# Loads in the order of need, weights behind block 2, eight blocks of lookahead, mask building interleaved: sliding-window attention with a highway layer

## The chip, the cores and the metric

The kernel runs on one core of one Trainium2 chip. The metric is the device time of one execution in microseconds (us). A run also has a span, the time from its first to its last instruction in the trace; here it is about 1.7 us shorter than the device time. Every execution is labelled fast or slow; on one core, slow means over 1.5% above the fastest execution of the same kernel. Medians are over all executions, which takes in three slow ones: one of e5 and two of the kernel before beside e9 to e12.

Engines: PE does matmuls (PEld is its weight load), DVE is the vector engine, ACT the scalar engine, POOL (Pool in the text) the engine that here issues all loads but the small bias row, SP the one that issues the stores. A load is issued by an instruction and lands later, when the trace shows its data complete. PE is called cold where four transposes take 0.61 to 0.63 us in these traces, and warm where they take 0.39 to 0.40 us.

## The reference, cut to what matters

```python
# q, k, v: [4, 8, 768, 64] float32; n_sink = 4, window = 128
scores = q @ k^T / 8
keep   = (key < 4) | (0 <= query - key < 128)       # four sink keys and a window of 128
a      = softmax(where(keep, scores, -1e9))
x      = (a @ v) as [3072, 512]                      # tokens x (8 heads x 64)
H      = relu(x @ w_h)                               # w_h, w_t: [512, 512]
T      = sigmoid(x @ w_t + b_t)
out    = T * H + (1 - T) * x                         # float32
```

## The kernel before

The 3072 tokens are 24 blocks of 128. A load moves 128 tokens of all heads of q, k or v from float32 in memory to float16 on the chip (128 KB written); each weight is 512 KB. In the main loop PE, DVE and ACT follow the program's order (`manual_schedule`); Pool's queue, and everything in front of the loop, is ordered by the scheduler of the framework.

```python
sd_pool = ctx.enter_context(tc.tile_pool(name="p_sd", bufs=6))      # q and k as loaded
NV = 6
v_ring = [const.tile([P, VW], FP16, tag=f"v{i}") for i in range(NV)]  # VW = 8*65 + 64 = 584

load(0)                                   # q and k of block 0
make_identity(nc, ident)                  # on Pool
for vt in v_ring:
    nc.vector.memset(vt, 2.0)             # DVE; column 64 of each head stays 2.0 (row sums)
load_v(0); load(1)
nc.gpsimd.memset(mask, 1.0)               # then two affine_select on Pool, copies on DVE
...
load_v(1)
nc.gpsimd.dma_start(out=wt_sb, in_=moe_w_t...)    # both weights
nc.gpsimd.dma_start(out=wh_sb, in_=moe_w_h...)
... # bias row, sink helpers: small DVE and Pool work

with tc.manual_schedule(engines={ENG.PE, ENG.DVE, ENG.Activation}):
    for i in range(-2, NB + 1):
        if 2 <= i + 4 < NB:
            load(i + 4); load_v(i + 4)
        s = i + 1
        ... stage_sink(i)       # sink scores, for even i
        ... stage_S(s)          # scores of block s: PE, exponential on ACT
        ... stage_A(i)          # probabilities x v of block i
        ... stage_T(i + 2)      # PE transposes q and k, ACT copies qT, DVE copies kT
        ... stage_mask(s)       # DVE
        ... stage_Mt(i - 1)     # x @ w_t, tanh
        ... stage_X(i)          # transposes x
        ... stage_sink_setup
        ... stage_Mh(i - 1)     # x @ w_h, the rest of the highway layer, store
```

T(n), S(n), A(n), Mt(n) and Mh(n) below are these stages for block n; q2 is the q load of block 2, and so on. In PE's order, block 2 is transposed right after A(0), block 3 after A(1), and Mt(0) and Mh(0), the first users of the weights, follow T(3).

The softmax here doesn't subtract the row's maximum and nothing guards it: scores larger than these inputs give would overflow.

Of the kernel before, what the change touches and what calls it, by code (L numbers as in the profile page):

```python
# [9 lines left out]
FP16 = mybir.dt.float16  # L10
FP32 = mybir.dt.float32
AF = mybir.ActivationFunctionType
ALU = mybir.AluOpType
ENG = mybir.EngineType
# [7 lines left out]
def kernel(  # L22
# [18 lines left out]
    nc = tc.nc  # L41
    P = 128

    B, H, S, D = q.shape
    NSINK = int(n_sink)
# [4 lines left out]
    NT, DM = out.shape  # L50
# [4 lines left out]
    NB = NT // P  # L55
    NHP = H // 2
    NOC = DM // P
    SCALE = 1.0 / math.sqrt(D)
    VW = H * 65 + 64

    const = ctx.enter_context(tc.tile_pool(name="const", bufs=1))
    sd_pool = ctx.enter_context(tc.tile_pool(name="p_sd", bufs=6))
    qkT_pool = ctx.enter_context(tc.tile_pool(name="p_qkT", bufs=5))
    e_pool = ctx.enter_context(tc.tile_pool(name="p_e", bufs=5))
    es_pool = ctx.enter_context(tc.tile_pool(name="p_es", bufs=2))
# [5 lines left out]
    av_ps = ctx.enter_context(tc.tile_pool(name="ps_av", bufs=1, space=bass.MemoryType.PSUM))  # L71
    m_ps = ctx.enter_context(tc.tile_pool(name="ps_m", bufs=2, space=bass.MemoryType.PSUM))

    NV = 6
    v_ring = [const.tile([P, VW], FP16, tag=f"v{i}", name=f"v{i}") for i in range(NV)]
    qk_sd = {}

    def load(n):
        b, c = divmod(n, NSC)
        rows = slice(c * P, (c + 1) * P)  # L80
        qsd = sd_pool.tile([P, H, D], FP16, tag="qsd", name="qsd")
        ksd = sd_pool.tile([P, H, D], FP16, tag="ksd", name="ksd")
        nc.gpsimd.dma_start(out=qsd, in_=q[b, :, rows, :].transpose([1, 0, 2]))  # L83
        nc.gpsimd.dma_start(out=ksd, in_=k[b, :, rows, :].transpose([1, 0, 2]))  # L84
        qk_sd[n] = (qsd, ksd)

    def load_v(n):
        b, c = divmod(n, NSC)
        rows = slice(c * P, (c + 1) * P)
        vt = v_ring[n % NV][:, 0:H * 65].rearrange("p (h e) -> p h e", e=65)  # L90
        nc.gpsimd.dma_start(out=vt[:, :, 0:D], in_=v[b, :, rows, :].transpose([1, 0, 2]))
# [1 line left out]

    ebias = const.tile([P, 1], FP32, tag="ebias")
    nc.vector.memset(ebias, _EXP_BIAS)
    load(0)
    ident = const.tile([P, P], FP16, tag="ident")
    make_identity(nc, ident)
    for vt in v_ring:
        nc.vector.memset(vt, 2.0)  # L100
    load_v(0)
    load(1)


    mask = const.tile([P, 2, P], FP16, tag="mask", name="mask")
    nc.gpsimd.memset(mask, 1.0)
    nc.gpsimd.affine_select(
        out=mask[:, 1, :], in_=mask[:, 1, :], compare_op=ALU.is_ge, fill=0.0,
        base=0, pattern=[[1, P]], channel_multiplier=-1)
    nc.gpsimd.affine_select(  # L110
        out=mask[:, 0, :], in_=mask[:, 0, :], compare_op=ALU.is_ge, fill=0.0,
        base=-1, pattern=[[-1, P]], channel_multiplier=1)

    mask1 = const.tile([P, 2, P], FP16, tag="mask1", name="mask1")
    nc.vector.tensor_copy(out=mask1, in_=mask)
    nc.vector.memset(mask1[0:NSINK, 0, :], 1.0)
    mask0 = const.tile([P, P], FP16, tag="mask0", name="mask0")
    nc.vector.tensor_copy(out=mask0, in_=mask[:, 1, :])
    nc.vector.memset(mask0[0:NSINK, :], 1.0)

    load_v(1)
    wh_sb = const.tile([P, NOC, DM], FP16, tag="wh")
    wt_sb = const.tile([P, NOC, DM], FP16, tag="wt")
    nc.gpsimd.dma_start(out=wt_sb, in_=moe_w_t.rearrange("(kc p) of -> p kc of", p=P))
    nc.gpsimd.dma_start(out=wh_sb, in_=moe_w_h.rearrange("(kc p) of -> p kc of", p=P))


    bt32 = const.tile([1, DM], FP32, tag="bt32")
# [11 lines left out]
    for hh in range(2):  # L140
        nc.vector.tensor_copy(
            out=sel[:, :, 4 * hh:4 * hh + NSINK],
            in_=ident[:, 0:NSINK].unsqueeze(1).to_broadcast([P, NHP, NSINK]))
    bdm = const.tile([P, H], FP32, tag="bdm")
    nc.gpsimd.memset(bdm, 1.0)
    bdm3 = bdm.rearrange("p (a b) -> p a b", b=2)
    nc.gpsimd.affine_select(
        out=bdm3, in_=bdm3, compare_op=ALU.is_ge, fill=0.0,
        base=0, pattern=[[-32, NHP], [-4, 2]], channel_multiplier=1)
    nc.gpsimd.affine_select(  # L150
        out=bdm3, in_=bdm3, compare_op=ALU.is_ge, fill=0.0,
        base=NSINK - 1, pattern=[[32, NHP], [4, 2]], channel_multiplier=-1)
    ks_bd = []
    for i in range(2):
        t = const.tile([P, NHP * 160], FP16, tag=f"ks{i}", name=f"ks{i}")
# [11 lines left out]
    def stage_T(n):  # L167
        qsd, ksd = qk_sd.pop(n)
        tp = m_ps.tile([P, 2 * NHP, P], FP16, tag="m", name="tp")
        for j in range(NHP):  # L170
            nc.tensor.transpose(tp[:, j, :], qsd[:, 2 * j:2 * j + 2, :], ident)  # L171
        for j in range(NHP):
            nc.tensor.transpose(tp[:, NHP + j, :], ksd[:, 2 * j:2 * j + 2, :], ident)  # L173
        qT = qkT_pool.tile([P, NHP, P], FP16, tag="qT", name="qT")
        kT = qkT_pool.tile([P, NHP, P], FP16, tag="kT", name="kT")
        nc.scalar.copy(out=qT, in_=tp[:, 0:NHP, :])  # L176
        nc.vector.tensor_copy(out=kT, in_=tp[:, NHP:2 * NHP, :])  # L177
        qkT[n] = (qT, kT)

    def stage_sink_setup(b):  # L180
# [8 lines left out]
        vps = av_ps.tile([P, 2, 512], FP32, tag="av", name="vps")  # L189
        vt = v_ring[(b * NSC) % NV]  # L190
        for g in range(2):
# [11 lines left out]
    def stage_sink(n):  # L203

        b = n // NSC
        ks = ks_bd[b % 2]
        sk = m_ps.tile([P, 2, P], FP32, tag="m", name="sk")
        for t in range(2):
            qT, _ = qkT[n + t]
            for hp in range(NHP):  # L210
                nc.tensor.matmul(sk[:, t, :], lhsT=ks[:, hp * P:(hp + 1) * P],  # L211
                                 rhs=qT[:, hp, :], start=(hp == 0), stop=(hp == NHP - 1))
        es = es_pool.tile([P, 2, P], FP16, tag="es", name="es")
        nc.scalar.activation(out=es, in_=sk, func=AF.Exp, bias=ebias, scale=SCALE)  # L214
        es_of[n] = es_of[n + 1] = es

    def stage_S(n):
        c = n % NSC
        qT, kT = qkT[n]
        srcs = ([] if c == 0 else [qkT[n - 1][1]]) + [kT]  # L220
        np_ = len(srcs)
        es = []
        for g in range(2):
            sps = s_ps.tile([P, 2, 512], FP32, tag="s", name="sps")
            for hl in range(2):
                hp = 2 * g + hl
                for pc, kk in enumerate(srcs):
                    for hh in range(2):
                        rows = slice(64 * hh, 64 * hh + 64)
                        o = (hl * np_ + pc) * P  # L230
                        nc.tensor.matmul(sps[:, hh, o:o + P], lhsT=kk[rows, hp, :],  # L231
                                         rhs=qT[rows, hp, :], start=True, stop=True)
            e = e_pool.tile([P, 2, 2, np_, P], FP16, tag="e", name="e")
            nc.scalar.activation(out=e.rearrange("p a b c d -> p a (b c d)"),  # L234
                                 in_=sps[:, :, 0:2 * np_ * P], func=AF.Exp,
                                 bias=ebias, scale=SCALE)
            es.append(e)
        e_of[n] = (es, np_)

    def stage_mask(n):  # L240
        c = n % NSC
        es, np_ = e_of[n]
        m = {0: mask0, 1: mask1.rearrange("p a b -> p (a b)")}.get(
            c, mask.rearrange("p a b -> p (a b)"))
        for e in es:
            ev = e.rearrange("p a b c d -> p (a b) (c d)")
            nc.vector.tensor_tensor(  # L247
                out=ev, in0=ev, in1=m.unsqueeze(1).to_broadcast([P, 4, np_ * P]),
                op=ALU.mult)

    def stage_A(n):
        b, c = divmod(n, NSC)
        es, np_ = e_of.pop(n)
        vts = ([] if c == 0 else [v_ring[(n - 1) % NV]]) + [v_ring[n % NV]]
        av = av_ps.tile([P, 2, 4, P], FP32, tag="av", name="av")
# [66 lines left out]

    with tc.manual_schedule(engines={ENG.PE, ENG.DVE, ENG.Activation}):
        for i in range(-2, NB + 1):
            if 2 <= i + 4 < NB:
                load(i + 4)
                load_v(i + 4)
            s = i + 1
            if 0 <= i < NB and i % NSC >= 2 and i % 2 == 0:
                stage_sink(i)  # L330
            if 0 <= s < NB:
                stage_S(s)
            if 0 <= i < NB:
                stage_A(i)
            if i + 2 < NB:
                stage_T(i + 2)
            if 0 <= s < NB:
                stage_mask(s)
            if 0 <= i - 1 < NB:
                stage_Mt(i - 1)  # L340
            if 0 <= i < NB:
                stage_X(i)
            if 0 <= i < NB and i % NSC == 0:
                stage_sink_setup(i // NSC)
            if 0 <= i - 1 < NB:
                stage_Mh(i - 1)
# [35 lines left out]
```

## Time and profile before

| | before |
|---|---|
| time, median of 3 runs | 144.44 us (144.27 to 144.75) |
| span of the profiled run | 143.0 us |
| PE / DVE / ACT / Pool busy | 80 / 80 / 63 / 47% of the span |
| a block in the steady part | 4.85 us (29.1 us per six blocks) |

First the page of the kernel before: the span in 40 slices of 3.6 us, each digit the busy share in tenths.

```profile
PE   0345046999999969999999699999997999999730
DVE  6825007588989899989898999899889998999690
DMA  1999999999999998999999999999869021011111
```

PE and DVE stand mostly at 8 or 9 from slice 9 on: from there the blocks follow each other at the pace of the engines. Counted from 1, the hole is in slice 5 for PE and in slices 5 and 6 for DVE: PE stands from 13.4 to 19.1 us, DVE from 14.3 to 21.2 us. The DMA row stands at 9 for most of the span, which looks like a kernel bound by its loads, but that row says only that the DMA engines had work, and the waits have to say whether anybody stood still for it.

The second view is PE's timeline of the kernel before: start, duration, engine, line, instruction, out<-in, number merged; in brackets the idle time before it and what ended it.

```profile
4.87 0.61 PE L171 MATMUL tp<-ident,qsd 128*128 128x128 f16 x4 [4.87 <-DMA qsd<-in_q_dram]
8.86 0.61 PE L231 MATMUL sps<-qT,kT 64*128 64x128 f16 x8 [1.93 <-DVE kT L177]
12.43 0.93 PE L262 MATMUL av<-v_91,e 128*128 128x112 f16 x8
19.10 0.61 PE L171 MATMUL tp<-ident,qsd 128*128 128x128 f16 x4 [5.74 <-DMA qsd<-in_q_dram]
...
26.99 1.44 PE L298 MATMUL tps<-wt_sb,xT 128*128 128x512 f16 x4
28.49 1.03 PE L310 MATMUL hps<-wh_sb,xT 128*128 128x512 f16 x4
```

After A(0) (the `av` line) PE waits 5.74 us for q2. Why q2 is late is in Pool's timeline of the kernel before, which shows when each load is issued:

```profile
6.53 0.91 POOL L91 DMA_DIRECT2D v_92<-in_v_dram  x1
...
7.91 0.79 POOL L124 DMA_DIRECT2D wt_sb<-in_moe_w_t_dram  x1
8.68 0.77 POOL L125 DMA_DIRECT2D wh_sb<-in_moe_w_h_dram  x1
...
9.45 0.92 POOL L83 DMA_DIRECT2D qsd<-in_q_dram  x1
...
10.50 0.94 POOL L84 DMA_DIRECT2D ksd<-in_k_dram  x1
```

Both weights are issued in front of q2. The trace has w_t landing 7.4 us and w_h 9.5 us after issue, so q2 follows at 19.1 us. The last view is DVE's timeline of the kernel before:

```profile
1.03 0.55 DVE L100 MEMSET v_91<- 128x584 f16 x1
...
4.11 0.55 DVE L100 MEMSET v_96<- 128x584 f16 x1
...
7.78 0.27 DVE L118 COPY mask_126<-mask 128x128 f16<-128x128 f16 x1 [1.12 <-POOL mask L107]
...
8.45 0.35 DVE L177 COPY kT<-tp 128x512 f16<-128x512 f16 x1
```

Six memsets of v buffers, 0.615 us from start to start, and other constants stand in front of the first copy of kT, which releases the first scores at 8.86 us.

The chain of waits of the kernel before, followed back from its end, has the columns start, duration, and what the time went to. Three of its lines:

```profile
10.50 9.38 DMA ksd<-in_k_dram
...
60.51 1.11 ACT e L234
...
89.61 1.11 ACT e L234
```

The first is the one long stretch of DMA in it, the wait behind the weights. The other two are the same ACT exponential, six blocks apart, 29.1 us, with no load in the chain between them: in the steady part nobody waits for loads.

### The profile page before, as it was taken

What the parts mean: (1) busy time and instruction counts of PE and PEld (TensorE: products, weight loads), DVE (VectorE), ACT (ScalarE), POOL (GpSimd) and SP (SyncE); (2) the same over time, 40 slices, a digit from 0 to 9 for tenths busy, and PEclk for the clock granted to TensorE, in tenths of its full rate; (3) what the DMA queues carried; (4) which work ended last, traced back from release to release, by engine and by line L of the source; (5) the groups of instructions that cost most, each with busy time, mean ns of one, the idle gap of its engine ahead of it and who ended that gap; (6) DMA issues with size and microseconds to landing.
All of it is one profiled execution on the core that took longest, in us unless ns stands there. A gap on an engine that the chain in (4) does not pass through costs nothing.

```text
span 143.0 us, 3308 instructions
## 1 busy us (share of the span) xinstructions
PE 114.4 (80%) x1312; PEld 73.8 (52%) x1312; DVE 114.1 (80%) x228; ACT 90.3 (63%) x129; POOL 66.8 (47%) x86
## 2 busy tenths in 40 slices
PE   0345046999999969999999699999997999999730
PEld 0134034775676525756765366567644656675310
DVE  6825007588989899989898999899889998999690
ACT  3056026187787677779766867887759579774310
POOL 6999569719975744376349424753040000000000
PEclk9999999999999999999999999999999999999996
DMA  1999999999999998999999999999869021011111
GB/s 10 112 126 156 161 155 155 155 112 142 150 179 201 163 181 64 155 153 137 131 153 125 160 100 135 146 138 134 113 101 124 0 78 73 14 64 73 73 73 73
DMA packets 79408, 16.98 MB, mean 119 GB/s; under 512 B 75297, under 2 KB 76321, under 8 KB 79394
## 3 DMA queue, kind: packets, MB, share of 16 engines
q0 software_dynamic: 75936, 10.49, 109.1%
q1 hardware_dynamic: 3458, 6.30, 12.7%
q8 instruction: 10, 0.16, 0.4%
q14 instruction: 4, 0.03, 0.1%
HBM read 20.97 MB, written 6.29 MB: 191 GB/s over the span
## 4 chain that ended last, share of the span: by engine, by line
DVE 36%; PE 32%; ACT 10%; DMA 7%; issue 7%; POOL 6%; DVEq 0%; POOLq 0%
PE hps L310 12%; DMA ksd<-in_k_dram 7%; DVE ee L316 6%; DVE otok L319 6%; DVE e L247 6%; DVE dd L313 5%; ACT e L234 5%; DVE xh L277 5%; PE av L262 4%; PE tps L298 4%; PE xtp L286 3%; DVE kT L177 3%; PE sk L211 3%; ACT qT L176 2%; DVE vs L196 2%
## 5 line engine op out<-in xcount | busy, mean ns | idle before, releaser
L234 ACT ACTIVATE e<-sps,ebias 128x1024 f16<-128x1024 f32 (+1 forms) x48 | 47.4, 1039 | 15.7 <-PE sps L231 11.4
L298 PE MATMUL tps<-wt_sb,xT 128*128 128x512 f16 x96 | 25.1, 384 | 0.0
L310 PE MATMUL hps<-wh_sb,xT 128*128 128x512 f16 x96 | 24.6, 378 | 0.6
L83 POOL DMA_DIRECT2D qsd<-in_q_dram x24 | 21.9, 914 | 2.7 <-PE tp L173 1.7
L176 ACT COPY qT<-tp 128x512 f16<-128x512 f16 x24 | 14.0, 585 | 14.1 <-PE tp L173 14.1
L84 POOL DMA_DIRECT2D ksd<-in_k_dram x24 | 22.0, 916 | 2.0 <-DMA wh_sb<-in_moe_w_h_dram 2.0
L262 PEld LDWEIGHTS <-e 128*128 128x128 f16 x352 | 20.4, 100 | 4.2 <-DVE vs L196 1.2
L247 DVE TENSOR_TENSOR e<-e,mask 128x1024 f16<-128x1024 f16 x32 | 20.5, 682 | 0.0
L301 ACT ACTIVATE u<-tps 128x512 f16<-128x512 f32 x24 | 14.4, 600 | 9.0 <-PE tps L298 9.0
L177 DVE COPY kT<-tp 128x512 f16<-128x512 f16 x24 | 10.0, 418 | 12.0 <-ACT qT L176 12.0
L313 DVE SCALAR_TENSOR_TENSOR dd<-hps,xh 128x512 f16<-128x512 f32 x24 | 16.5, 687 | 3.4 <-PE hps L310 3.4
L316 DVE SCALAR_TENSOR_TENSOR ee<-u,dd 128x512 f16<-128x512 f16 x24 | 16.6, 692 | 2.9 <-ACT es L214 0.5
L171 PE MATMUL tp<-ident,qsd 128*128 128x128 f16 x96 | 10.2, 234 | 10.6 <-DMA qsd<-in_q_dram 10.6
L231 PE MATMUL sps<-qT,kT 64*128 64x128 f16 x352 | 15.2, 228 | 2.8 <-DVE kT L177 2.1
L319 DVE SCALAR_TENSOR_TENSOR otok<-xh,ee 128x512 f32<-128x512 f16 x24 | 16.6, 692 | 0.8
L277 DVE TENSOR_TENSOR xh<-av,rec 128x512 f16<-128x512 f32 x24 | 16.6, 691 | 0.8
L231 PEld LDWEIGHTS <-kT 64*128 64x128 f16 x352 | 10.7, 99 | 10.1 <-issue 6.8
L288 ACT COPY xT<-xtp 128x512 f16<-128x512 f16 x24 | 14.0, 583 | 1.2 <-PE xtp L286 0.7
L298 PEld LDWEIGHTS <-xT 128*128 128x128 f16 x96 | 9.6, 100 | 9.1 <-issue 0.8
L310 PEld LDWEIGHTS <-xT 128*128 128x128 f16 x96 | 9.2, 97 | 8.1 <-issue 1.3
L171 PEld LDWEIGHTS <-qsd 128*128 128x128 f16 x96 | 7.4, 104 | 11.2 <-DMA qsd<-in_q_dram 10.8
L286 PEld LDWEIGHTS <-xh 128*128 128x128 f16 x96 | 6.2, 100 | 13.1 <-DVE xh L277 11.5
(66 smaller groups left out, 161.8 us busy)
## 6 DMA issues: line engine op xcount, KB each, us to landing
out_dram<-otok SPq DMA_DIRECT2D x24, 256.0 KB, 2.6
qsd<-in_q_dram POOLq DMA_DIRECT2D x24, 128.0 KB, 4.9
ksd<-in_k_dram POOLq DMA_DIRECT2D x24, 128.0 KB, 5.3
v_91<-in_v_dram POOLq DMA_DIRECT2D x4, 128.0 KB, 4.2
v_92<-in_v_dram POOLq DMA_DIRECT2D x4, 128.0 KB, 3.9
wt_sb<-in_moe_w_t_dram POOLq DMA_DIRECT2D x1, 512.0 KB, 7.4
wh_sb<-in_moe_w_h_dram POOLq DMA_DIRECT2D x1, 512.0 KB, 9.5
v_93<-in_v_dram POOLq DMA_DIRECT2D x4, 128.0 KB, 5.3
```

Source lines behind the costliest of these rows:

```text
L83: nc.gpsimd.dma_start(out=qsd, in_=q[b, :, rows, :].transpose([1, 0, 2]))
L84: nc.gpsimd.dma_start(out=ksd, in_=k[b, :, rows, :].transpose([1, 0, 2]))
L231: nc.tensor.matmul(sps[:, hh, o:o + P], lhsT=kk[rows, hp, :], rhs=qT[rows, hp, :], start=True, stop=True)
L234: nc.scalar.activation(out=e.rearrange("p a b c d -> p a (b c d)"), in_=sps[:, :, 0:2 * np_ * P], func=AF.Exp, bias=ebias, scale=SCALE)
L247: nc.vector.tensor_tensor(out=ev, in0=ev, in1=m.unsqueeze(1).to_broadcast([P, 4, np_ * P]), op=ALU.mult)
L262: nc.tensor.matmul(av[:, g, 2 * hl + hh, 0:_AVN], lhsT=es[g][:, hh, hl, pc, :], rhs=vt[:, 65 * h:65 * h + _AVN], start=first, stop=False, ...
L277: nc.vector.tensor_tensor(out=xh, in0=avh[:, :, 0:D], in1=rec.unsqueeze(2).to_broadcast([P, H, D]), op=ALU.mult)
L298: nc.tensor.matmul(tps, lhsT=xT[:, kc, :], rhs=wt_sb[:, kc, :], start=False, stop=(kc == NOC - 1))
L310: nc.tensor.matmul(hps, lhsT=xT[:, kc, :], rhs=wh_sb[:, kc, :], start=(kc == 0), stop=(kc == NOC - 1))
L313: nc.vector.scalar_tensor_tensor(out=dd, in0=hps, scalar=0.0, in1=xh, op0=ALU.max, op1=ALU.subtract)
L316: nc.vector.scalar_tensor_tensor(out=ee, in0=u, scalar=1.0, in1=dd, op0=ALU.add, op1=ALU.mult)
L319: nc.vector.scalar_tensor_tensor(out=otok, in0=xh, scalar=2.0, in1=ee, op0=ALU.mult, op1=ALU.add)
```

## The change

The intent: no block should wait behind data that is needed later. Weights go between blocks 2 and 3, the lookahead grows from four blocks to eight, the mask building is spread between the loads, and the constant fills of the identity and the mask move from Pool to DVE.

```diff
+    AHEAD = 8
-    sd_pool = ctx.enter_context(tc.tile_pool(name="p_sd", bufs=6))
+    sd_pool = ctx.enter_context(tc.tile_pool(name="p_sd", bufs=AHEAD))
-    NV = 6
+    NV = AHEAD + 3
@@ start
-    load(0)
-    make_identity(nc, ident)
+    nc.vector.memset(ident, 1.0)
+    nc.vector.memset(mask, 1.0)
     for vt in v_ring:
         nc.vector.memset(vt, 2.0)
-    load_v(0)
-    load(1)
-    nc.gpsimd.memset(mask, 1.0)
-    (two affine_select of mask)
-    load_v(1)
-    nc.gpsimd.dma_start(out=wt_sb, ...)
-    nc.gpsimd.dma_start(out=wh_sb, ...)
+    with tc.manual_schedule(engines={ENG.Pool}):
+        load(0)
+        (affine_select of ident)
+        load_v(0)
+        load(1)
+        (affine_select of mask[:, 1, :])
+        load_v(1)
+        (affine_select of mask[:, 0, :])
+        load(2)
+        nc.gpsimd.dma_start(out=wt_sb, ...)
+        load_v(2)
+        load(3)
+        nc.gpsimd.dma_start(out=wh_sb, ...)
+        load_v(3)
+        (bdm, a constant for the sinks)
+        for n in range(4, AHEAD):
+            load(n)
+            load_v(n)
@@ main loop
-            if 2 <= i + 4 < NB:
-                load(i + 4)
-                load_v(i + 4)
...
             if i + 2 < NB:
                 stage_T(i + 2)
+            if i + 2 + AHEAD < NB:
+                load(i + 2 + AHEAD)
+                load_v(i + 2 + AHEAD)
```

More of the change, by code (lines that the diff above doesn't have):

```diff
@@ L95 @@
     nc.vector.memset(ebias, _EXP_BIAS)
-    load(0)
+    wh_sb = const.tile([P, NOC, DM], FP16, tag="wh")
+    wt_sb = const.tile([P, NOC, DM], FP16, tag="wt")
     ident = const.tile([P, P], FP16, tag="ident")
-    make_identity(nc, ident)
+    mask = const.tile([P, 2, P], FP16, tag="mask", name="mask")
+    nc.vector.memset(ident, 1.0)
+    nc.vector.memset(mask, 1.0)
     for vt in v_ring:
         nc.vector.memset(vt, 2.0)
-    load_v(0)
-    load(1)
-    mask = const.tile([P, 2, P], FP16, tag="mask", name="mask")
@@ L106 @@
-    nc.gpsimd.memset(mask, 1.0)
-    nc.gpsimd.affine_select(
-        out=mask[:, 1, :], in_=mask[:, 1, :], compare_op=ALU.is_ge, fill=0.0,
-        base=0, pattern=[[1, P]], channel_multiplier=-1)
-    nc.gpsimd.affine_select(
-        out=mask[:, 0, :], in_=mask[:, 0, :], compare_op=ALU.is_ge, fill=0.0,
-        base=-1, pattern=[[-1, P]], channel_multiplier=1)
+    with tc.manual_schedule(engines={ENG.Pool}):
+        load(0)
+        nc.gpsimd.affine_select(
+            out=ident, in_=ident, compare_op=ALU.is_equal, fill=0.0,
+            base=0, pattern=[[-1, P]], channel_multiplier=1)
+        load_v(0)
+        load(1)
+        nc.gpsimd.affine_select(
+            out=mask[:, 1, :], in_=mask[:, 1, :], compare_op=ALU.is_ge, fill=0.0,
+            base=0, pattern=[[1, P]], channel_multiplier=-1)
+        load_v(1)
+        nc.gpsimd.affine_select(
+            out=mask[:, 0, :], in_=mask[:, 0, :], compare_op=ALU.is_ge, fill=0.0,
+            base=-1, pattern=[[-1, P]], channel_multiplier=1)
+        load(2)
+        nc.gpsimd.dma_start(out=wt_sb, in_=moe_w_t.rearrange("(kc p) of -> p kc of", p=P))
+        load_v(2)
+        load(3)
+        nc.gpsimd.dma_start(out=wh_sb, in_=moe_w_h.rearrange("(kc p) of -> p kc of", p=P))
+        load_v(3)
+        bdm = const.tile([P, H], FP32, tag="bdm")
+        nc.gpsimd.memset(bdm, 1.0)
+        bdm3 = bdm.rearrange("p (a b) -> p a b", b=2)
+        nc.gpsimd.affine_select(
+            out=bdm3, in_=bdm3, compare_op=ALU.is_ge, fill=0.0,
+            base=0, pattern=[[-32, NHP], [-4, 2]], channel_multiplier=1)
+        nc.gpsimd.affine_select(
+            out=bdm3, in_=bdm3, compare_op=ALU.is_ge, fill=0.0,
+            base=NSINK - 1, pattern=[[32, NHP], [4, 2]], channel_multiplier=-1)
+        for n in range(4, AHEAD):
+            load(n)
+            load_v(n)
@@ L114 @@
+    mask0 = const.tile([P, P], FP16, tag="mask0", name="mask0")
+    nc.vector.tensor_copy(out=mask0, in_=mask[:, 1, :])
+    nc.vector.memset(mask0[0:NSINK, :], 1.0)
     mask1 = const.tile([P, 2, P], FP16, tag="mask1", name="mask1")
@@ L116 @@
     nc.vector.memset(mask1[0:NSINK, 0, :], 1.0)
-    mask0 = const.tile([P, P], FP16, tag="mask0", name="mask0")
-    nc.vector.tensor_copy(out=mask0, in_=mask[:, 1, :])
-    nc.vector.memset(mask0[0:NSINK, :], 1.0)
-    load_v(1)
-    wh_sb = const.tile([P, NOC, DM], FP16, tag="wh")
-    wt_sb = const.tile([P, NOC, DM], FP16, tag="wt")
-    nc.gpsimd.dma_start(out=wt_sb, in_=moe_w_t.rearrange("(kc p) of -> p kc of", p=P))
-    nc.gpsimd.dma_start(out=wh_sb, in_=moe_w_h.rearrange("(kc p) of -> p kc of", p=P))
     bt32 = const.tile([1, DM], FP32, tag="bt32")
@@ L143 @@
             in_=ident[:, 0:NSINK].unsqueeze(1).to_broadcast([P, NHP, NSINK]))
-    bdm = const.tile([P, H], FP32, tag="bdm")
-    nc.gpsimd.memset(bdm, 1.0)
-    bdm3 = bdm.rearrange("p (a b) -> p a b", b=2)
-    nc.gpsimd.affine_select(
-        out=bdm3, in_=bdm3, compare_op=ALU.is_ge, fill=0.0,
-        base=0, pattern=[[-32, NHP], [-4, 2]], channel_multiplier=1)
-    nc.gpsimd.affine_select(
-        out=bdm3, in_=bdm3, compare_op=ALU.is_ge, fill=0.0,
-        base=NSINK - 1, pattern=[[32, NHP], [4, 2]], channel_multiplier=-1)
     ks_bd = []
```

## The prediction

> **What bounds the kernel now.** Two different things. In the steady part (chain of waits, about 30 to 130 us) the chain runs through PE, DVE and ACT work only, with a period of 29.1 us per six blocks (60.51 to 89.61, and 88.60 to 117.88), 4.85 us a block; no load is in it, although the DMA row says 99% there. A block's three loads take 3 x 0.88 us of Pool issue and land 4 to 5 us after issue, so loads keep ahead. The start is bound by loads: in the timeline, PE ends A(0) at 13.36 and stands idle 5.74 us until q of block 2 lands (transposes at 19.10, k at 19.93). Both weights (issued 7.91 and 8.68, landing 7.4 and 9.5 us later) are in front of block 2. The other early bound is DVE: from 0.87 to 8.45 it fills constants (six v memsets, 0.615 us apart; 1.12 us waiting for Pool's mask), and only then copies kT(0), which releases the first scores at 8.86.
>
> **What the change does.**
> - Loads of block 2 go before the weights. Counting Pool's instructions (0.88 us a load, 0.3 a select), q2 is issued near 7.7 and k2 near 8.6, and they land near 12 (3.5 to 4 us later). Removes the 5.74 us gap.
> - With about 0.85 us per 128 KB load (landings after 18.2 us) and about 3.9 us per weight (7.8 us between the landing of v1 and of wh), estimates: wt 16.2, k3 18.8, wh 22.7, k4 25.2. Needs, if everything after T(2) moves by 3.7 us: T(3) near 22, w_t near 23.3, w_h near 24.8, T(4) near 27.7. So no new load stall, margin of w_h about 2 us.
> - Costs: v ring 6 -> 11 adds five v memsets (5 x 0.615 = 3.1 us) plus ident and mask memsets on DVE (384 elements, about 0.4 us). The Trainium skill, "VectorE: DVE Perf Modes", Zero memsets can be issued as uint32, says one cycle an element whatever the type; the trace agrees (545 ns for 584 elements). The mask wait (1.12 us) disappears under them. kT(0) moves from 8.45 to about 10.8, so everything up to A(0) starts about 2.35 us later: this is on the critical path and eats part of the gain.
> - Eight blocks ahead instead of four: worth nothing, since no load waits in the steady part. Fewer Pool memsets: nothing.
>
> **Sum.** A(0) ends near 15.7 instead of 13.36; T(2) follows at once; kT(2), 21.19 before, comes near 17.4 to 17.6. Gain about 3.7 us, carried to the end because the steady period stays 4.85 us a block. Matmuls of 24 to 28 us ran cold (300 ns against 212 later); without the gap the PE may warm earlier (the Trainium skill, "TensorE: Matmul & The Clock Gate", What's actually happening: a window of about 3.4 us of activity). I count 0.3 us for that. 144.44 - 4.0 = 140.4 us, range 138.6 to 142.3. Chances: faster 0.77, same 0.22, slower 0.01.
>
> **What would show it.** Idle before T(2) below 0.5 us; 11 v memsets in a row on DVE and kT(0) near 10.8 us; T(2) near 15.7; no wait of PE for qsd, ksd or the weights after 12 us; steady period 29.1 us; DMA row at 9 in the first slices, then lower.
>
> **What would make it wrong.** If the memsets of later v tiles don't stand before kT(0) on DVE, the gain nears 5.7 us. If the weights land later than estimated, Mh(0) waits and the gain shrinks. If the clock warms well before A(1), up to 1.5 us more.

## The result, and the profile after

| | before | after |
|---|---|---|
| time, median of 4 runs | 144.57 us (144.27 to 144.75) | 140.34 us (139.75 to 140.70) |
| ratio of the fast runs | | 0.9705, 95% interval 0.9664 to 0.9746 |
| span of the profiled run | 143.0 us | 139.0 us |
| T(2) starts | 19.10 us | 15.03 us |
| first exponential of sink scores | 30.00 us | 25.99 us |

A ratio here is the mean time of one kernel's fast runs over that of the other's in the same rounds, so it is not quite the ratio of the medians. The change is faster by 3%. The same rows of the page after:

```profile
PE   0306879999999699999999699999996999999730
DVE  6895466689988999899898999898989998999590
DMA  1999999999999999999999959221011021101111
```

The hole of PE in slice 5 is gone. A smaller one opens in slice 3: there PE waits 3.74 us for the first kT copy (1.93 us before), while DVE, busy with its constants, stands at 9, where it stood at 2. DMA falls off after slice 25 instead of slice 31: the loads are done earlier, with nothing to show for it. PE's timeline after (blocks 0 to 3 and the first use of each weight):

```profile
4.85 0.61 PE L182 MATMUL tp<-ident,qsd 128*128 128x128 f16 x4 [4.85 <-DMA qsd<-in_q_dram]
10.73 0.61 PE L242 MATMUL sps<-qT,kT 64*128 64x128 f16 x8 [3.74 <-DVE kT L188]
...
15.03 0.63 PE L182 MATMUL tp<-ident,qsd 128*128 128x128 f16 x4
...
22.48 1.91 PE L309 MATMUL tps<-wt_sb,xT 128*128 128x512 f16 x4
...
24.48 1.03 PE L321 MATMUL hps<-wh_sb,xT 128*128 128x512 f16 x4
```

T(2) has no wait in brackets any more. Pool's timeline after:

```profile
7.59 0.92 POOL L84 DMA_DIRECT2D qsd<-in_q_dram  x1
8.47 0.91 POOL L85 DMA_DIRECT2D ksd<-in_k_dram  x1
9.34 0.79 POOL L122 DMA_DIRECT2D wt_sb<-in_moe_w_t_dram  x1
...
14.35 0.98 POOL L92 DMA_DIRECT2D v_99<-in_v_dram  x1
...
15.39 1.00 POOL L92 DMA_DIRECT2D v_100<-in_v_dram  x1
...
17.85 0.91 POOL L84 DMA_DIRECT2D qsd<-in_q_dram  x1 [1.23 <-DMA wt_sb<-in_moe_w_t_dram]
```

q2 and k2 are in front of w_t. But two loads in front of the last line were not expected: `v_99` and `v_100` are the ninth and tenth v buffers, so these are v of blocks 8 and 9, and they go in front of q4, the last line. In the main loop Pool's queue is not held to the program's order, and eleven v buffers let the scheduler pull them forward. The bracket says that Pool then stood idle 1.23 us until w_t had landed, before it issued q4; why this load waits for that one is not shown by any run here. DVE's timeline after:

```profile
7.60 0.55 DVE L104 MEMSET v_101<- 128x584 f16 x1
...
10.33 0.35 DVE L188 COPY kT<-tp 128x512 f16<-128x512 f16 x1
10.61 0.46 DVE L144 COPY mask_176<-mask 128x256 f16<-128x256 f16 x1
```

The eleventh memset starts at 7.60 us, and the first kT copy comes at 10.33 us, 1.88 us later than before. A(0) therefore starts at 14.31 us instead of 12.43 us. The 5.74 us of the gap minus these 1.88 us are 3.86 us; T(2) starts 4.07 us earlier, since it now follows A(0) in PE's pipeline, 0.72 us after A(0)'s start, and no longer after its modelled end 0.93 us behind it. The small wait for k2 (0.22 us) went too, and the third kT copy on DVE, which needs k2, comes 4.45 us earlier (16.74 instead of 21.19 us). The chain of waits after:

```profile
7.60 0.55 DVE v_101 L104
...
56.51 1.11 ACT e L245
...
85.63 1.11 ACT e L245
```

No DMA is left in this chain; its first 10 us are DVE's constants, of which the first line is one. The exponential is again 29.1 us apart for six blocks, and both are 4.0 us earlier than before.

That the rest of the kernel only moves is the most useful number. From the first exponential of the sink scores (30.00 us before, 25.99 us after) to the end of the span it is 113.0 us in both.

### The profile page after: what moved, and what is told of

Its sections match the earlier page's. It is cut to its first block, busy times and chain, and to the rows that moved or that the text cites. A ratio compares the mean times of both kernels' runs of the same rounds, so it can differ in the third digit from the quotient of the medians.

```text
span 139.0 us, 3303 instructions
## 1 busy us (share of the span) xinstructions
PE 114.6 (82%) x1312; PEld 74.1 (53%) x1312; DVE 117.2 (84%) x235; ACT 90.4 (65%) x129; POOL 66.2 (48%) x84
## 4 chain that ended last, share of the span: by engine, by line
DVE 42%; PE 33%; ACT 14%; issue 8%; DVEq 0%
PE hps L321 12%; ACT e L245 9%; DVE ee L327 6%; DVE otok L330 6%; DVE e L258 6%; DVE dd L324 6%; DVE xh L288 5%; PE av L273 4%; PE tps L309 4%; DVE kT L188 4%; PE xtp L297 3%; ACT qT L187 3%; PE sps L242 3%; PE sk L222 3%; DVE vs L207 2%
## 5 line engine op out<-in xcount | busy, mean ns | idle before, releaser
L84 POOL DMA_DIRECT2D qsd<-in_q_dram x24 | 21.5, 895 | 5.3 <-DMA wt_sb<-in_moe_w_t_dram 1.2
L85 POOL DMA_DIRECT2D ksd<-in_k_dram x24 | 21.4, 890 | 2.3 <-DMA wh_sb<-in_moe_w_h_dram 1.2
L297 PE MATMUL xtp<-ident,xh 128*128 128x128 f16 x96 | 9.7, 225 | 4.2 <-DVE xh L288 4.2
```

The lines of the kernel that those rows point to most:

```text
L84: nc.gpsimd.dma_start(out=qsd, in_=q[b, :, rows, :].transpose([1, 0, 2]))
L85: nc.gpsimd.dma_start(out=ksd, in_=k[b, :, rows, :].transpose([1, 0, 2]))
```

## The experiments

Twelve runs were made: ten new kernels (e1 to e10), the changed kernel again (e11) and e8 again (e12). Besides the times, this table gives milestones from the one profiled execution of each: T(2), T(3), the first sink exponential (es) and the span. Span minus es is 112.9 to 113.2 us in every one of them except e4 (116.8) and e9 (114.4), where block 4 is waited for behind es; so the column es tells what the start cost. The profiled execution need not be a typical one: those of the changed kernel, e2, e4, e7, e9, e10 and e11 were the slowest of their runs.

| kernel | median us | ratio to before | T(2) | T(3) | es | span |
|---|---|---|---|---|---|---|
| before | 144.44 | 1 | 19.10 | 25.71 | 30.00 | 143.0 |
| after | 140.34 | 0.9705 | 15.03 | 21.21 | 25.99 | 139.0 |
| e1_order_only | 140.34 | 0.9715 | 13.19 | 20.04 | 25.01 | 138.0 |
| e2_weights_first | 144.81 | 1.001 | 19.10 | 25.72 | 30.98 | 144.0 |
| e3_ahead4 | 139.38 | 0.9651 | 13.16 | 19.51 | 24.71 | 137.7 |
| e4_small_memset | 140.66 | 0.9753 | 13.10 | 19.05 | 23.56 | 140.4 |
| e5_deep_only | 144.85 | 1.0019 | 18.93 | 25.72 | 29.63 | 142.6 |
| e6_more_memsets | 143.13 | 0.9856 | 17.99 | 23.48 | 28.21 | 141.2 |
| e7_small_pool_in_order | 139.40 | 0.9594 | 12.57 | 19.01 | 25.23 | 138.4 |
| e8_need_order | 139.12 | 0.9585 | 12.55 | 18.91 | 23.78 | 136.9 |
| e11_after_again | 140.37 | 0.973 | 15.04 | 21.27 | 26.41 | 139.5 |
| e9_after_warm | 140.88 | 0.9745 | 14.65 | 20.63 | 25.08 | 139.5 |
| e12_need_order_again | 138.57 | 0.9608 | 12.27 | 18.18 | 24.07 | 137.0 |
| e10_need_order_warm | 137.73 | 0.9537 | 12.50 | 18.75 | 23.35 | 136.3 |

e1 to e4 shared their runs of the kernel before (median 144.68 us), e5 to e8 theirs (145.03 us), e9 to e12 theirs (144.57 us). Each group ran on another chip. Across these groups, compare ratios.

The theory: the gain is the place of the weights alone, and DVE's longer run of memsets takes part of it back. The main rival: the lookahead makes the gain, because the DMA row is full.

### e1_order_only: the order alone, in the kernel before

```diff
-    nc.gpsimd.dma_start(out=wt_sb, ...)
-    nc.gpsimd.dma_start(out=wh_sb, ...)
@@ main loop of the kernel before, after load(i + 4)
+                if i == -2:
+                    nc.gpsimd.dma_start(out=wt_sb, ...)
+                if i == -1:
+                    nc.gpsimd.dma_start(out=wh_sb, ...)
```

> The kernel before with one edit: w_t is issued after q and k of block 2, w_h after q and k of block 3; four blocks ahead, six v buffers and the old masks stay. Theory (the gain is the load order, and the longer memset run of the change eats part of it): PE transposes block 2 at about 13.4 us instead of 19.1 us, the first k copy on DVE stays at about 8.5 us, total about 138.8 us (138.2 to 139.8), faster than the changed kernel; a wait of up to 0.7 us for w_h is possible. Rival (the gain is the eight blocks of lookahead, since the DMA row stands at 99%): about 144 us.

Measured: 140.34 us (139.52 to 141.36), ratio 0.9715. The rival falls: with four blocks of lookahead and the old masks, the order gives all that the change gives. T(2) came at 13.19 us as expected, without a wait, but the total missed its range by 0.5 us. In the profiled run (139.75 us, within the range) one part of the shortfall is visible in PE's timeline:

```profile
13.19 0.63 PE L169 MATMUL tp<-ident,qsd 128*128 128x128 f16 x4
...
20.04 0.61 PE L169 MATMUL tp<-ident,qsd 128*128 128x128 f16 x4 [0.42 <-DMA qsd<-in_q_dram]
20.88 0.60 PE L171 MATMUL tp<-ident,ksd 128*128 128x128 f16 x4 [0.23 <-DMA ksd<-in_k_dram]
```

Once the start is shorter, block 3's loads are the next to be late, by 0.65 us together. Why two of the four executions were slower still (140.93 and 141.36 us) is not known: only the profiled one has a trace.

### e2_weights_first: the changed kernel with the weights back in front of block 2

```diff
-        load(2)
-        nc.gpsimd.dma_start(out=wt_sb, ...)
+        nc.gpsimd.dma_start(out=wt_sb, ...)
+        nc.gpsimd.dma_start(out=wh_sb, ...)
+        load(2)
         load_v(2)
         load(3)
-        nc.gpsimd.dma_start(out=wh_sb, ...)
```

> The changed kernel with only the weights put back in front of block 2; eight blocks ahead, interleaved masks and eleven v buffers stay. Theory: block 2 lands at about 19 us again, PE idles about 3.5 us before it, total 144.4 us (143.8 to 145.0), same as before. Rival (lookahead or mask interleaving made the gain): about 141 us.

Measured: 144.81 us, ratio 1.001 (0.997 to 1.0051), with this wait in front of T(2):

```profile
19.10 0.61 PE L182 MATMUL tp<-ident,qsd 128*128 128x128 f16 x4 [3.93 <-DMA qsd<-in_q_dram]
```

Lookahead and interleaved masks without the order are worth nothing. The wait is 3.93 us and not 5.74 us because DVE's memsets now delay A(0), but T(2) starts at the same 19.10 us: here those memsets are hidden behind the late block.

### e5_deep_only: deeper buffers alone, in the kernel before

```diff
-    sd_pool = ctx.enter_context(tc.tile_pool(name="p_sd", bufs=6))
+    sd_pool = ctx.enter_context(tc.tile_pool(name="p_sd", bufs=8))
-    NV = 6
+    NV = 11
```

> The kernel before with only deeper buffers: eight q and k buffers and eleven v buffers, so that the load queue may run further ahead; order of loads and masks as before. Theory: block 2 still stands behind the weights, the longer v memset run on DVE hides behind that wait, total as before, 144.5 us (144.0 to 145.2). Rival (lookahead made the gain): about 141 us.

Measured: 144.85 us, ratio 1.0019 (0.9932 to 1.0107), as the theory has it; one of its four executions was slow (146.75 us) and is not in the ratio. Three kernels now agree: e1 has the order without the lookahead and gains, e2 and e5 have the lookahead without the order and don't.

### e6_more_memsets: five more memsets on DVE in the changed kernel

```diff
     for vt in v_ring:
         nc.vector.memset(vt, 2.0)
+    spare = const.tile([P, VW], FP16, tag="spare", name="spare")
+    for _ in range(5):
+        nc.vector.memset(spare, 2.0)
```

> The changed kernel with five more memsets of 584 elements (3.1 us of DVE work) into a tile that nobody reads, placed with the v memsets. Theory: DVE's run of memsets stands in front of the first k copy and the loads have slack in that direction, so the whole of it shows: first k copy at about 13.5 to 14 us instead of 10.3, total 143.4 us (142.9 to 144.2). Rival (DVE's constants are off the critical path): 140.3 us.

Measured: 143.13 us, ratio 0.9856 against 0.9705 of the changed kernel; the first kT copy at 13.28 us, 2.95 us later, and T(2) at 17.99 us, 2.96 us later, for 3.08 us of memsets. So DVE's constants stand on the critical path nearly one for one in this direction. The span grew by 2.2 us only. The other 0.7 us were won back between T(2) and T(3), where PE was warm earlier in this run: the two `vps` matmuls took 0.39 us together instead of 0.59 us, and the 16 matmuls of the scores behind them 0.62 us instead of 1.03 us.

### e3_ahead4: the changed kernel with four blocks of lookahead

```diff
-    AHEAD = 8
+    AHEAD = 4
```

> The changed kernel with AHEAD = 4 (four q and k buffers, seven v buffers). Theory: the four v memsets that fall away (2.46 us on DVE) stand before the first k copy, which moves from 10.3 to about 7.9 us; total about 138.0 us (137.4 to 138.9), and no load wait in the steady part. Rival (lookahead matters): slower than the changed kernel, 141 to 144 us.

Measured: 139.38 us (139.04 to 140.04), ratio 0.9651. It is no slower than the changed kernel, and its span minus es is 113.0 us too, so the lookahead is again worth nothing. The median is 1 us lower instead of the expected 2.3 us, above its range, and the intervals of the two ratios overlap (0.9610 to 0.9692 against 0.9664 to 0.9746). The first kT copy moved from 10.33 to 7.72 us, as expected. In the trace the gain shrinks on the way, in part at loads that had been hidden: PE waits 0.26 us for q1 and 0.23 us for k1, and 2.61 us at the first kT copy are 1.86 us at the second; T(3) starts 1.70 us earlier, PE waits 0.23 us for k3, and es is 1.28 us earlier.

### e4_small_memset: fill only what no load writes

```diff
     for vt in v_ring:
-        nc.vector.memset(vt, 2.0)
+        nc.vector.memset(vt[:, 0:H * 65].rearrange("p (h e) -> p h e", e=65)[:, :, D:D + 1], 2.0)
+        nc.vector.memset(vt[:, H * 65:VW], 2.0)
```

> The changed kernel, but each v buffer is filled only where no load writes: the eight ones columns and the 64 columns of padding, 72 elements instead of 584. Theory: DVE's run before the first k copy shrinks by about 4.5 us, so the copy is then bound by the landing of k0 and by ACT's q copy and comes at about 7.7 us instead of 10.3; total about 137.9 us (137.2 to 138.8), with waits of some tenths for k2 or w_h. Rival (memsets are off the critical path): 140.3 us, as the changed kernel.

Measured: 140.66 us (140.31 to 142.13), ratio 0.9753: no gain over the changed kernel, although the first kT copy came at 7.63 us as expected, T(3) at 19.05 us and the first sink exponential 2.43 us earlier than in the changed kernel. It was given back right after that. PE's timeline of this run:

```profile
26.55 0.40 PE L183 MATMUL tp<-ident,qsd 128*128 128x128 f16 x4 [1.34 <-DMA qsd<-in_q_dram]
27.41 0.40 PE L185 MATMUL tp<-ident,ksd 128*128 128x128 f16 x4 [0.46 <-DMA ksd<-in_k_dram]
...
29.42 1.91 PE L322 MATMUL hps<-wh_sb,xT 128*128 128x512 f16 x4
```

Block 4 is late by 1.34 and 0.46 us, and after that pause PE runs cold: the four matmuls with w_h take 1.91 us instead of about 1.03 us. This execution was the slowest of the four. Two of the others had a mean granted clock (the share of PE's full clock that the profile shows as granted) of 0.990, against 0.966 here, and took 140.65 and 140.31 us, still no less than the changed kernel; so the loss does not need the cold stretch. In the changed kernel, with the same queue of loads, T(4) starts at 27.47 us, only about 1 us after q4 landed (26.5 us in both traces); the margin there was thin.

### e7_small_pool_in_order: the same with Pool held to the program's order

```diff
-    with tc.manual_schedule(engines={ENG.PE, ENG.DVE, ENG.Activation}):
+    with tc.manual_schedule(engines={ENG.PE, ENG.DVE, ENG.Activation, ENG.Pool}):
```

> As the run with small memsets, but the Pool queue keeps the program's order in the main loop too, so that the v loads of blocks 8 and 9 no longer go in front of q of block 4. Theory (what ate the gain of the small memsets was the arrival of block 4, 1.8 us of waits and a cold clock behind it): block 4's transposes start without a wait of more than 0.5 us, total 138.5 us (137.9 to 139.3). Rival (the gain of the memsets is lost elsewhere, on k of block 1 and so on, and the order of block 4 is of no matter): 140.5 us.

Measured: 139.40 us (138.26 to 140.15), ratio 0.9594 (0.9527 to 0.9660) against 0.9753 (0.9693 to 0.9813) without this line. T(4) started without a wait:

```profile
26.71 0.39 PE L183 MATMUL tp<-ident,qsd 128*128 128x128 f16 x4
```

That alone says little, because PE came to it later than in e4 (es at 25.23 against 23.56 us). The landings decide: q4 landed at about 24.7 us instead of 26.5 us, and k4 at 25.6 instead of 27.3 us. So the two v loads that had been pulled forward did delay block 4 by about 1.8 us, and the rival falls. The total is 0.1 us above the expected range. In the profiled execution, the slowest of the four, block 3 is now the one that is late (0.83 and 0.28 us of wait), and PE is cold behind it: the four matmuls with w_h take 1.73 us, against 1.03 us in e4.

### e8_need_order and e12_need_order_again: loads in the order of PE's first use

```diff
-    AHEAD = 8
+    AHEAD = 6
     (small memsets and Pool in order, as in the run before)
     load(0)
-    load_v(0)
     load(1)
-    load_v(1)
+    load_v(0)
     load(2)
-    nc.gpsimd.dma_start(out=wt_sb, ...)
-    load_v(2)
+    load_v(1)
     load(3)
+    nc.gpsimd.dma_start(out=wt_sb, ...)
     nc.gpsimd.dma_start(out=wh_sb, ...)
-    load_v(3)
+    load_v(2)
+    load(4)
+    load_v(3)
+    load(5)
+    load_v(4)
+    load_v(5)
```

> A version meant to beat both: small memsets, six blocks ahead, Pool in program order, loads in the order of first use by PE: q0 k0 q1 k1 v0 q2 k2 v1 q3 k3 w_t w_h v2 q4 k4 v3. Theory (with the DVE run short, arrivals of k1, of block 3 and of block 4 set the start): block 2 is transposed near 12.5 us, block 3 near 18.4 us, total 137.6 us (136.8 to 138.7). Rival (only the place of the weights against block 2 counts): as the run before it.

> The version with small memsets and loads in the order of first use once more, beside the changed kernel on the same chip. Expected 1.2 us (0.7 to 2.0) less than the changed kernel of the same rounds, ratio to the kernel before about 0.960. Rival (its first run only met a slow run of the kernel before): within 0.4 us of the changed kernel.

Measured: 139.12 us, ratio 0.9585, in the first, above its range; 138.57 us (138.06 to 139.70), ratio 0.9608 (0.9561 to 0.9655), in the second, beside the changed kernel at 140.37 us in the same rounds. It beats the changed kernel by 1.8 us of medians. That is the whole package, though. Against e7, in the same rounds, the finer order brought nothing that can be told from noise (0.9585, 0.9530 to 0.9641, against 0.9594, 0.9527 to 0.9660), so the rival, "as the run before it", stands. No load of q or k is waited for after 7 us in either trace. What waits now is Mh(0): in the second run PE stood 1.79 us for w_h.

```profile
22.55 1.04 PE L322 MATMUL hps<-wh_sb,xT 128*128 128x512 f16 x4 [1.79 <-DMA wh_sb<-in_moe_w_h_dram]
```

In the first run it did not wait: w_h landed at about 22.2 us, and PE came to it only at 22.26 us, since T(3) started later (18.91 against 18.18 us) and the w_t matmuls took longer (1.80 against 1.08 us).

> The changed kernel once more, unchanged, so that the three runs beside it are compared on one chip in the same rounds. Expected ratio to the kernel before 0.970 (0.967 to 0.974), as in its first run.

The changed kernel came out at 140.37 us (140.11 to 141.21), ratio 0.973 (0.9688 to 0.9771), inside the range of its expectation.

### e9_after_warm and e10_need_order_warm: spare matmuls on PE while it is idle

```diff
+    warm = const.tile([P, P], FP16, tag="warm", name="warm")
+    nc.vector.memset(warm, 1.0)
+    def warm_up(count):
+        wps = s_ps.tile([P, 2, 512], FP32, tag="s", name="wps")
+        for _ in range(count):
+            nc.tensor.matmul(wps[:, 0, 0:P], lhsT=warm, rhs=warm, start=True, stop=True)
@@ in front of the main loop
+        warm_up(36)
@@ in the loop, after stage_T
+            if i == -2:
+                warm_up(32)      # 10 in e10_need_order_warm
```

> The changed kernel with spare matmuls of 128x128 on PE (36 in front of the first transposes, 32 in the idle time behind them), which write a PSUM tile that nobody reads. They test the clock term of the prediction: if PE is warm from about 5 us on, the matmuls of the start take 212 ns instead of 300 ns. The prediction's upper guess: 1.5 us less than the changed kernel beside it. Rival (the start is set by DVE, ACT and the loads, and PE's speed there is worth little): within 0.4 us of it, or slower by the 0.17 us of the extra memset.

Measured: 140.88 us (140.22 to 141.16) beside 140.37 us: no gain. First the row of the granted clock on this run's page, in tenths of full speed, then PE's timeline.

```profile
PEclk9999559999999999999999999999999999999996
```

```profile
6.51 2.25 PE L339 MATMUL wps<-warm 128*128 128x128 f16 x32
...
11.18 0.40 PE L184 MATMUL tp<-ident,qsd 128*128 128x128 f16 x4
...
14.65 0.63 PE L184 MATMUL tp<-ident,qsd 128*128 128x128 f16 x4
...
23.56 1.04 PE L323 MATMUL hps<-wh_sb,xT 128*128 128x512 f16 x4 [0.79 <-DMA wh_sb<-in_moe_w_h_dram]
...
27.37 0.40 PE L184 MATMUL tp<-ident,qsd 128*128 128x128 f16 x4 [0.64 <-DMA qsd<-in_q_dram]
```

The clock did warm: four transposes take 0.40 us at 11.18 us. It fell again (0.63 us at 14.65 us; the clock row shows 5 in slices 5 and 6), although PE's longest pause in between was 2.09 us. Still T(3) started at 20.63 instead of 21.27 us in the rerun of the changed kernel beside it. That time was then spent waiting: 0.79 us for w_h, 0.64 us for q4 and 0.46 us for k4. A faster PE met the next loads sooner, but these loads were also later here than in e11: w_h landed at 23.5 instead of 21.5 us, q4 at 27.3 instead of 25.2 us and k4 at 28.1 instead of 26.5 us, with Pool idle 2.29 us for w_t in front of q4. Whether the spare matmuls made them late is not shown. So the test says that warming PE in this way brings the changed kernel nothing, and not what a warm PE alone would be worth.

> The version with small memsets and loads in the order of first use, with spare matmuls on PE (36 in front of the first transposes, 10 behind them). If PE's cold clock is what now sets the start: blocks 1 to 3 come closer together, 1 to 1.5 us less than the same version without them, about 137.7 us, unless the landing of block 3's loads or of w_h takes its place, then 0.3 to 0.8 us less. Rival (PE's speed is worth little there): within 0.3 us.

Measured: 137.73 us (137.13 to 138.05), ratio 0.9537 (0.9498 to 0.9576), the best of all, 0.84 us of medians less than the same loads without spare matmuls (0.9608, 0.9561 to 0.9655; the intervals overlap by 0.0015, but each of its six executions was faster than each of the six without). Its first sink exponential comes at 23.35 us. That the clock made this is not shown: in the profiled run the transposes of block 1 still took 0.61 us for four, so PE was cold there, and T(3) came later than in e12 (18.75 against 18.18 us). What the trace shows is a shorter wait for w_h, 0.25 us instead of 1.79 us: it landed 9.9 us after issue instead of 10.5 us.

## Why the prediction was right

The prediction gave 140.4 us and a range of 138.6 to 142.3 us; 140.34 us was measured. Point by point:

- **The weights in front of block 2 are the cost: right.** The 5.74 us gap went, T(2) has no wait, and e1, e2 and e5 show that the order alone does it.
- **DVE's longer memset run is on the path and takes part of the gain: right, a little too large.** It predicted 2.35 us and 1.88 us was measured. The difference lies in two things: the bias scaling took 0.41 us instead of 0.72 us, and the second mask copy ran behind the first kT copy (10.61 after 10.33 us) and no longer in front of it. A memset of 256 elements took 0.27 us on DVE both as float16 and as uint32, so the number of elements set the cost, as the prediction assumed. e6 shows the one-for-one cost, e3 and e4 the same from the other side.
- **Lookahead worth nothing in the steady part: right** (e3, e5). The steady period stayed at 29.1 us per six blocks, and span minus es is 113.0 us with four blocks (e3) as with eight.
- **The clock term: wrong sign in the profiled pair, and not a property of the change.** It counted 0.3 us of gain from an earlier warm clock. In the profiled run the first four matmuls with w_t took 1.91 us, against 1.44 us before (the `tps` lines above). The lead is 4.5 us at T(3) (25.71 against 21.21) and 4.0 us at the first sink exponential. The Trainium skill, "TensorE: Matmul & The Clock Gate", What's actually happening, says that the window is free-running, and the spread fits that: in two executions of one program the same matmuls took 1.80 us (e8_need_order) and 1.08 us (e12_need_order_again).
- **The two errors cancel, by luck.** The third kT copy came about 0.7 us earlier than predicted (16.74 us against 17.4 to 17.6), the clock took about 0.5 us instead of giving 0.3. The total is closer than the terms.
- **Margins of the later loads: right that nothing waits, optimistic in size.** It foresaw w_t at 16.2 us and w_h at 22.7 us (they landed near 17.2 and 22.3, issue plus 7.9 and 9.6 us), and k4 at 25.2 us, which landed near 27.1 us, 0.5 us before its transposes. It missed that v of blocks 8 and 9 would be issued in front of q4. This cost nothing in the changed kernel, but in e4 it took back most of the gain, as e7 shows.

## What to carry to other kernels

Do not let large loads that are needed later stand in front of the load that the critical engine waits for; a full DMA row said nothing about this here, the wait in front of one instruction did. A finer order of first use was not shown to bring more (e8 against e7). When a start-up wait went, the next one was only 1 or 2 us behind it (here DVE's constants, then k of block 1, then blocks 3 and 4, then w_h), so look at the milestone where the steady part begins. Deeper buffers were not free: each v buffer cost 0.615 us of memset in front of the first use, and more of them let the scheduler pull later loads in front of those that were needed next.

## What the Trainium skill lacked or had wrong

- "DMA: Bandwidth & Descriptors", Anatomy of one DMA, calls descriptor generation "small, variable" in its table. Here each 128 KB load of 1024 short rows held Pool for about 0.88 us, and the first six loads of the kernel before were issued 1.04 us apart with the mask work between them (1.31 to 6.53 us). Its fit (2.0 us plus bytes over 436 GB/s) would give an estimate of 2.3 us for 128 KB; the very first load took 3.5 us from issue to landing. Whether the short rows make the difference was not tested.
- "TensorE: Matmul & The Clock Gate", What's actually happening, has the clock go cold after an idle window of about 3.4 us. In e9_after_warm PE was warm at 13.4 us (14 matmuls of the scores in 0.56 us), the granted clock fell at about 13.9 us, and PE was cold at 14.65 us, with no pause of PE over 2.09 us since it had warmed. The page's part on PSUM-queue cycling tells of short pauses that do this, but gives no length of pause.
- The same page warns that clock events in traces are unreliable, but does not tell of what is seen here. In these traces the first cold stretch is not in the granted clock at all: it reads 1.00 from 20 to 30 us in the kernel before, where the matmuls on v took 300 ns until 25.6 us and 212 ns after 30 us. Later falls are recorded (0.84 from 20 to 30 us in e4_small_memset).
